# Another order for the 418 tasks of the first stage of an attention and two-layer MoE kernel

## The chip, the cores and the metric

The kernel runs on one core of a Trainium2 chip. The metric is the time of one execution on the device in microseconds; the number before is the median of 3 runs. One further execution was recorded by the hardware profiler; all rows below come from it.

## The reference

Attention with a window (plain for the first half of the heads, dilated by 4 for the second), its output as the input of a gated layer, whose output goes through a second layer with a leaky activation. All in float32.

```python
def _attn_ref(q, k, v):                        # 4 batches, 8 heads, 576 rows, 64 columns
    scores = scale * np.matmul(q, k.transpose(0, 1, 3, 2))
    ...                                        # window 32; heads 4 to 7: window 128, every 4th
    attn = np.exp(scores - np.max(scores, axis=-1, keepdims=True))
    attn = attn / (np.sum(attn, axis=-1, keepdims=True) + 1e-09)
    return np.matmul(attn, v)

def _moe_ref(x, w_gate, w_val, w_out):         # x: 2304 x 512, inner width 1536
    gate = 1.0 / (1.0 + np.exp(-(x @ w_gate)))
    return gate * (x @ w_val) @ w_out

def _moe2_ref(x, w_in, w_out, alpha):          # inner width 2048
    h = x @ w_in
    g = np.maximum(h, 0.0) + alpha * np.minimum(h, 0.0)
    return g @ w_out
```

## The kernel before

A large product is done in float16 with two halves of each operand: a high half (the value scaled by a power of two and rounded to float16) and a low half (what is left). Three products, high x high, high x low and low x high, are summed in PSUM. Every weight is therefore prepared on the chip before TensorE can use it: its bits are put together, a bound of its rows is summed, a power of two is made of that, and high and low halves are written.

The kernel has a first stage, which is a text (`FIRST`, line 1562 on) of 418 tasks, and then loops over the batches b = 1 to 3 and over the second layer, with a planner (`prepare`) that puts the second layer's weights between their products. The first stage covers the attention of batch 0 (`hb` 0 and 1: plain and dilated heads), of batch 1 (`hb` 2 and 3) and the start of batch 2 (`hb` 4), all weights of the gated layer, its products for batch 0, and the first three gate and value blocks of batch 1.

Inside `tc.manual_schedule()` (line 1309 on) the order of the text is the order of the instructions: `run` walks through it and calls one function for each task, and each function issues instructions on one or several engines. Each engine works off its own queue strictly in the order of issue, and semaphores tie the queues together. So a task that stands earlier in the text stands earlier on every engine that it uses, and an instruction that waits holds all those behind it on its engine.

The tasks, with the engines on which they issue:

- `lqk hb`, `lv hb`, `lgv m`, `lo d r`: loads, issued by SP's queue (lines 246, 247, 252, 499, 532). `lgv m` loads 512 KB of gate and 512 KB of value weights. Words of weights and v share 8 slots (pool `yp`); a load waits on SP's queue until a slot comes free, and the loads behind it wait with it.
- `dec m`, `odec d r ...`: VectorE puts the words of a block together, three instructions for each 512 KB (lines 180, 184, 188); the last two read two SBUF tensors.
- `wb m`, `xb hb`, `obd d h`: ACT sums squares (line 195). `wsum`, `xsum`, `osum`, `alpha`: TensorE sums over partitions with a column of ones (line 149). `wpow`, `xpow`, `opow`: VectorE (157, 161) and GpSimd (165) make the power of two.
- `spl m i e`, `ospl d h e`: the two halves of a weight block. With e = 1, ACT writes the high half (172) and VectorE the low one (173). With e = 0 or none, ACT scales the source in place (205) and writes the high half (206), and GpSimd subtracts (169).
- `qkm hb c` (TensorE, 302 to 316), `qks` (VectorE), `exp` (ACT, 362 or 368), `rs` (VectorE), `pm hb c e` (row scaling of the probabilities, 381: GpSimd for e = 0, VectorE for 1), `tr` (VectorE, 399), `phi` (ACT, 403), `plo hb i e` (subtraction, 169, GpSimd for 0, VectorE for 1), `vhi` (ACT, 272), `vlo` (VectorE, 275), `pvm` and `pv32` (TensorE, 430 and 445), `pvx hb half pair` (ACT 172 and VectorE 173, the two halves of x).
- `g b m i`, `v b m i`: half i of the gate and the value product of block m and batch b on TensorE (582), 12 matmuls. `sig` (ACT, 595), `mul` (VectorE, 600), `half b m e` (ACT 610, then the subtraction 169 on GpSimd for 1 or none, on VectorE for 0).
- `orow d r e`: row scaling of w_out (199; GpSimd for e = 0, VectorE for 1). `o b d p`: a quarter of an output product on TensorE (627), 18 matmuls. `oy`: its way to DRAM. `wgs`, `gs`: small scalings on GpSimd (488). `warm n bank`: n products of zeros on TensorE.
- `prep n`: a call of the planner.

The two functions behind a split, and the one behind a half:

```python
    def split_weight(hi, lo, src, s, on_dve=0):                # line 201
        if on_dve:
            return split_act(hi, lo, src, s)                   # ACT 172, VectorE 173
        nc.scalar.activation(src, src, AF.Copy, scale=s)       # ACT 205
        nc.scalar.activation(hi, src, AF.Copy)                 # ACT 206
        rest(nc.gpsimd, lo, src, hi)                           # GpSimd 169

    def gv_halves(b, m, pool=True):
        ...
        nc.scalar.activation(t[:, 0, :], gf, AF.Copy)          # ACT 610
        rest(nc.gpsimd if pool else nc.vector, t[:, 1, :], gf, t[:, 0, :])
```

Of the kernel before, what the change touches and what calls it, by code (L numbers as in the profile page):

```python
# [1572 lines left out]
4; v 0 2 1; dec 5; g 0 3 0; qks 2 1; wpow 4; wb 5; wsum 5 0; g 0 3 1; qks 2 2; spl 4 0; spl 4 1 1; half 0 0 1; wpow 5;
mul 0 2; exp 2; v 0 3 0; dec 6; wgs 3; sig 0 3; v 0 3 1; xpow 1; spl 5 0 1; lgv 8; wb 6; spl 5 1 1; g 0 4 0; wsum 6; v
0 4 0; wgs 4; half 0 2 1; mul 0 3; lgv 10; wpow 6; spl 6 0; g 0 4 1; sig 0 4; spl 6 1; dec 7; wgs 5; g 0 5 0; wb 7;
half 0 3; v 0 4 1; wsum 7; rs 2; g 0 5 1; lgv 9; sig 0 5; wpow 7; g 0 6 0; mul 0 4; wgs 7; spl 7 0; pm 2; v 0 5 0; dec
8; v 0 5 1; tr 2; spl 7 1; g 0 6 1; wb 8; wgs 6; v 0 6 0; wsum 8; half 0 4; wpow 8; dec 9; sig 0 6; vhi 2; g 0 7 0;
mul 0 5; lv 4; phi 2; v 0 6 1; spl 8 0; lqk 3; g 0 7 1; plo 2; spl 8 1 1; wb 9; sig 0 7; lgv 11; mul 0 6; vlo 2; half
0 6 1; half 0 5 1; g 0 8 0; wsum 9 0; lo 0 2; v 0 7 0; lo 0 1; wpow 9; g 0 8 1; dec 10; pvm 2 0; pvx 2 0 1; spl 9 0;
spl 9 1 1; wgs 8; v 0 7 1; wb 10; wsum 10; mul 0 7; v 0 8 0; pvx 2 0 0; wpow 10; sig 0 8; dec 11; spl 10 0 1; spl 10  # L1580
1; v 0 8 1; g 0 9 0; half 0 7 1; wb 11; pvm 2 1; wsum 11; g 0 9 1; pvx 2 1 0; v 0 9 0; odec 0 0 1 2; wpow 11; wgs 9;
orow 0 0 0; v 0 9 1; lo 2 0; orow 0 1 1; pvx 2 1 1; spl 11 0; orow 0 2 0; lo 2 2; qkm 3 0; lo 1 1; qks 3 0; spl 11 1
1; qkm 3 1; mul 0 8; wgs 10; g 0 10 0; xb 4; vhi 3; obd 0 1; obd 0 0; odec 1 0 1; lo 3 1; osum 0; half 0 8 1; qkm 3 2;
sig 0 9; opow 0; v 0 10 0; g 0 10 1; mul 0 9; v 0 11 0; vlo 3; half 0 9 0; wgs 11; v 0 10 1; lo 1 2; odec 1 2; ospl 0
0 1; qks 3 2; qks 3 1; lo 2 1; orow 1 2 0; sig 0 10; lo 3 2; orow 1 0 1; mul 0 10; orow 1 1 0; v 0 11 1; g 0 11 0; g 0
11 1; ospl 0 1; obd 1 0; lqk 4; obd 1 1; osum 1; o 0 0 0; exp 3; odec 2 0 1 2; opow 1; sig 0 11; orow 2 2 0; orow 2 1
1; mul 0 11; orow 2 0 1; o 0 0 1; rs 3; ospl 1 0 1; half 0 11 1; obd 2 1; obd 2 0; pm 3; osum 2; ospl 1 1; o 0 0 2;
# [89 lines left out]
```

## Time and profile before

| | us |
|---|---|
| median of 3 runs | 870.41 (869.15 to 870.77) |
| span of the profiled execution | 870.0 |
| TensorE (PE) busy | 830.0 (95%) |
| VectorE (DVE) busy | 618.3 (71%) |
| ACT busy | 440.7 (51%) |
| GpSimd (POOL) busy | 286.7 (33%) |

"Busy" is the union of an engine's instruction spans. The profile gives the granted clock of TensorE as a share of full speed, which is 2.4 GHz; its other level is 1.2 GHz, so a mean of 0.93 over a stretch is 14% of its time at the low level. Matmuls overlap, so the time of a run of them is read from start to start. A group of instructions is listed with its line, the engine, the operation, the tiles (written<-read), shapes and count, its busy time and the mean of one, then the idle time of the engine just ahead of them and what ended it.

### The profile page before, as it was taken

To read this page: it belongs to the slowest core of one execution; us is meant where nothing else is said; L and a number is where in the kernel's file an instruction comes from. 1 tells how busy PE (TensorE), PEld (TensorE's weight loads), DVE (VectorE), ACT (ScalarE), POOL (GpSimd) and SP (SyncE) were. 2 spreads that over 40 slices of the span, in tenths; PEclk is the share of its full clock that TensorE was granted. 3 is DMA by queue.
4 is the path that set the end of the run, shared out by engine and by line. 5 is a ranking of instruction groups with operands and counts; after the bars stand their busy time and mean duration, and the time that the engine had idled before them with its cause. 6 is when DMAs were issued, how large, how long until landed. Compare 5 with 4: busy or idle time off the path is not lost.

```text
span 870.0 us, 21031 instructions
## 1 busy us (share of the span) xinstructions
PE 830.0 (95%) x8994; PEld 686.7 (79%) x8994; DVE 618.3 (71%) x1031; ACT 440.7 (51%) x730; POOL 286.7 (33%) x261
## 2 busy tenths in 40 slices
...
GB/s 323 286 194 124 229 100 207 15 173 102 92 95 169 139 136 119 50 68 264 301 166 223 342 214 221 337 241 218 308 203 212 243 210 194 225 309 194 122 230 73
DMA packets 85181, 166.91 MB, mean 192 GB/s; under 512 B 5344, under 2 KB 57696, under 8 KB 85088
## 3 DMA queue, kind: packets, MB, share of 16 engines
...
## 4 chain that ended last, share of the span: by engine, by line
PE 76%; DVE 13%; ACT 5%; DMA 4%; issue 2%; POOL 1%; SPq 0%; ACTq 0%; DVEq 0%
PE banks L582 27%; PE banks L1204 18%; PE banks L959 17%; PE banks L627 11%; DVE plain L188 2%; DVE plain L184 2%; DVE plain L180 2%; PE banks L430 1%; PE banks L316 1%; DMA words<-w_out 1%; DMA words<-w_gate 1%; ACT junk L195 1%; DVE plain L199 1%; DMA w_i<-wi_dram 1%; DVE g_g L1045 1%
## 5 line engine op out<-in xcount | busy, mean ns | idle before, releaser
L582 PE MATMUL banks<-xh,w_gv 128*128 128x288 f16 x2304 | 295.5, 290 | 3.1 <-DVE gf L600 2.3
L582 PEld LDWEIGHTS <-w_gv 128*128 128x128 f16 x2304 | 226.1, 99 | 63.3 <-issue 3.2
L959 PE MATMUL banks<-yh,w_i 128*128 128x256 f16 x1536 | 187.1, 273 | 5.1 <-DMA w_i<-wi_dram 1.6
L959 PEld LDWEIGHTS <-w_i 128*128 128x128 f16 x1536 | 150.0, 98 | 24.0 <-issue 3.3
L627 PE MATMUL banks<-gt,w_o 128*128 128x288 f16 x1152 | 147.0, 288 | 0.3 <-POOL gt L169 0.2
L627 PEld LDWEIGHTS <-w_o 128*128 128x128 f16 x1152 | 112.0, 98 | 29.4 <-issue 0.4
L1204 PEld LDWEIGHTS <-g_gv 128*128 128x128 f16 x780 | 76.3, 98 | 8.8
L1204 PE MATMUL banks<-w,g_gv 128*128 128x256 f16 x612 | 75.5, 273 | 0.0
L997 ACT ACTIVATE neg<-banks 128x512 f32<-128x512 f32 x72 | 42.8, 594 | 57.2 <-DVE banks L1017 40.8
L1055 POOL TENSOR_TENSOR yh<-temp_y 128x512 f32<-128x512 f32 x16 | 26.5, 1659 | 125.7 <-DVE temp_y L1005 121.0
L600 DVE SCALAR_TENSOR_TENSOR gf<-banks,sg 128x576 f32<-128x576 f32 x48 | 36.0, 751 | 38.9 <-PE banks L582 27.3
L165 POOL TENSOR_SCALAR sc<-sc 128x1 f32<-128x1 f32 x35 | 11.4, 326 | 157.7 <-DVE sc L161 157.7
L1204 PEld LDWEIGHTS <-g_g 128*128 128x128 f16 x564 | 55.2, 98 | 6.4
L169 POOL TENSOR_TENSOR gt<-gf,gt 128x576 f16<-128x576 f32 x24 | 36.8, 1533 | 63.5 <-ACT gt L610 63.3
L195 ACT ACTIVATE junk<-plain 128x1024 bf16<-128x1024 f32 (+1 forms) x36 | 36.2, 1006 | 40.3 <-DVE plain L199 28.3
L595 ACT ACTIVATE sg<-banks,sc 128x576 f32<-128x576 f32 x48 | 35.3, 735 | 38.1 <-PE banks L582 27.7
L610 ACT ACTIVATE gt<-gf 128x576 f16<-128x576 f32 x48 | 32.3, 676 | 41.3 <-DVE gf L600 41.3
L188 DVE SCALAR_TENSOR_TENSOR plain<-words,plain 128x512 uint32<-128x512 uint32 x68 | 50.8, 767 | 1.2
L184 DVE SCALAR_TENSOR_TENSOR plain<-words,plain 128x512 uint32<-128x512 uint32 x68 | 50.2, 759 | 1.2
L1204 PE MATMUL banks<-w,g_g 128*128 128x256 f16 x396 | 48.3, 273 | 0.0
L1005 DVE SCALAR_TENSOR_TENSOR temp_w<-neg,sc,banks 128x256 f32<-128x256 f32 x64 | 27.8, 475 | 25.1 <-ACT neg L997 25.1
L1045 DVE SCALAR_TENSOR_TENSOR g_gv<-temp_w,sc,g_gv 128x256 f16<-128x256 f32 (+1 forms) x37 | 26.0, 711 | 27.6 <-ACT g_gv L1041 27.6
...
## 6 DMA issues: line engine op xcount, KB each, us to landing
...
```

The source lines that it names most:

```text
L169: engine.tensor_tensor(out=lo, in0=src, in1=hi, op=ALU.subtract)
L184: nc.vector.scalar_tensor_tensor(out=d, in0=hi, scalar=0xC0000000, in1=d, op0=ALU.bitwise_and, op1=ALU.bitwise_or)
L188: nc.vector.scalar_tensor_tensor(out=d, in0=lo, scalar=29, in1=d, op0=ALU.logical_shift_right, op1=ALU.bitwise_or)
L195: nc.scalar.activation(junk[:, :src.shape[1]], src, AF.Square, accum_out=dst)
L582: nc.tensor.matmul(ps[:, h, :], lhsT=a, rhs=x_[:, H2 * h:H2 * h + H2], start=(kk == 0 and i == 0), stop=(kk == KD - 1 and i == 2),)
L595: nc.scalar.activation(halves(sg), ps, AF.Sigmoid, scale=sgx[b][:, m:m + 1])
L600: nc.vector.scalar_tensor_tensor(out=halves(gf), in0=ps, scalar=2.0 ** -15, in1=halves(sg), op0=ALU.mult, op1=ALU.mult)
L627: nc.tensor.matmul(ps[:, h, :], lhsT=a, rhs=x_[:, H2 * h:H2 * h + H2], start=(m == 0 and z == 0), stop=(m == M1 - 1 and z == 2),)
L959: nc.tensor.matmul(o, lhsT=h, rhs=l, start=(new and v == 0 and q == 1), stop=(q == total_), skip_group_check=True,)
L997: nc.scalar.activation(t[:, :2 * n], src[:, :2 * n], AF.Relu, scale=-1.0)
L1045: nc.vector.scalar_tensor_tensor(out=h[:, 1], in0=x_, scalar=s_al, in1=h[:, 0], op0=ALU.mult, op1=ALU.subtract)
L1204: nc.tensor.matmul(ps[:, H4 * t:H4 * t + H4].rearrange("p (c f) -> p c f", c=2), lhsT=a, rhs=x_, start=(first and k == 0 and t == 0 and z ...
```

## The change

`FIRST` gets another order. No other line of the kernel differs. Apart from the place, 39 of the 418 tasks change their engine argument:

- From GpSimd to VectorE: `spl` 0 0, 0 1, 1 0, 3 0, 3 1, 4 0, 6 0, 6 1, 7 0, 7 1, 8 0, 10 1, 11 0 (with one ACT instruction less each); `ospl` 0 1; `half` 0 0, 0 4, 0 5, 0 6, 0 7, 0 10, 1 1; `orow` 0 0, 0 2, 1 1, 3 0, 3 2; `plo` 1 1, 2, 3; `pm` 1 1.
- From VectorE to GpSimd: `spl` 1 1 and 4 1 (with one ACT instruction more each), `half` 0 9, `orow` 0 1.
- Written out but the same: `spl 9 0`, `half 0 3`, `ospl` 1 1 and 2 1, `plo 4`.

The text starts with the loads, decodes and bounds of weight blocks 0 and 1, which stood behind the loads of q, k and v before. `alpha` moves from ahead of `opow 3` to behind `pvx 3 1`, and some gate and value products of batch 1 (`g 1 2`) stand between the output products of batch 0.

The diff, cut:

```diff
 FIRST = """
-lqk 0 3; warm 6 2; warm 8 5; lqk 1 3; qkm 0 0; qks 0 0; qkm 0 1; exp 0 0; qks 0 1 1; qkm 0 2; lv 0; exp 0 1; lv 1; rs
-0 0; qks 0 2 1; qkm 1 0 4; exp 0 2; lgv 0; rs 0 1; pm 0 0 0; qks 1 0; pm 0 1 0; tr 0 0; exp 1 0; tr 0 1; rs 0 2; lal;
-xb 0; pm 0 2 0; lgv 1; lgv 3; qkm 1 1 5; qks 1 1; qkm 1 2 0; rs 1 0; lqk 2; exp 1 1; tr 0 2; pm 1 0 0; qks 1 2 1; rs 1
-1; xb 1; exp 1 2; pm 1 1 0; pv32 0 0 6; lgv 2; dec 0 0; xsum 0 0; rs 1 2; pm 1 2 0; xpow 0; tr 1 1; pv32 0 1 4; vhi 1;
-tr 1 0; phi 1 1; lv 3; dec 0 1; warm 14 3; plo 1 1; lgv 6; pvx 0 0 1; tr 1 2; pvx 0 0 0; wb 0; phi 1 2; vlo 1; lv 2;
-wsum 0; phi 1 0; pvx 0 1 0; plo 1 0 0; plo 1 2 0; wpow 0; pvm 1 0; pvx 0 1 1; dec 1; pvm 1 1 4; spl 0 0; pvx 1 1 1;
-spl 0 1; g 0 0 0; pvx 1 0 0; pvx 1 0 1; lgv 4; wb 1; wsum 1; qkm 2 0; wpow 1; pvx 1 1 0; spl 1 0; wgs 0; g 0 0 1; dec
-2; g 0 1 0; wgs 1; spl 1 1 1; lgv 5; dec 3; wb 2; v 0 0 0; wsum 2 0; sig 0 0; qkm 2 1; lgv 7; wpow 2; spl 2 0 1; spl 2
...
-0; lv 5; ospl 2 1; obd 3 1; o 0 1 2; oy 0 0; orow 3 0 0; o 0 2 0; orow 3 1 1; obd 3 0; pvm 3 0; o 0 1 3; osum 3;
-alpha; opow 3; pvx 3 0 1; o 0 2 1; pvx 3 0 0; pvm 3 1; ospl 3 0 1; pvx 3 1 0; ospl 3 1 1; o 0 3 0; o 0 2 2; pvx 3 1 1;
-qkm 4 0; oy 0 1; qkm 4 1; qks 4 0; qkm 4 2; qks 4 1; qks 4 2; o 0 2 3; o 0 3 1; g 1 0 0; prep 3; g 1 0 1; exp 4; o 0 3
...
+warm 6 2; lgv 0; dec 0 0; dec 0 1; wb 0; lgv 1; warm 8 5; dec 1; wb 1; lqk 0 3; qkm 0 0; qkm 0 1; wsum 0; qks 0 0; qkm
+0 2; lqk 1 3; qkm 1 0 4; wpow 0; qks 0 1 1; exp 0 0; qkm 1 1 5; qks 0 2 1; exp 0 1; rs 0 0; pm 0 0 0; lv 0; qks 1 0;
+wsum 1; rs 0 1; qks 1 1; lv 1; pm 0 1 0; qkm 1 2 0; wpow 1; exp 0 2; qks 1 2 1; exp 1 1; rs 0 2; exp 1 0; pm 0 2 0; tr
+0 1; xb 0; rs 1 0; tr 0 2; tr 0 0; lgv 2; pm 1 0 0; tr 1 0; warm 14 3; rs 1 1; pm 1 1 1; exp 1 2; lgv 3; lqk 2; rs 1
+2; xb 1; pm 1 2 0; lal; tr 1 1; xsum 0 0; lv 3; lgv 6; xpow 0; tr 1 2; spl 0 0 1; spl 0 1 1; pv32 0 0 6; vhi 1; phi 1
+0; vlo 1; pvx 0 0 1; pvx 0 0 0; lv 2; phi 1 1; plo 1 1 1; pv32 0 1 4; pvx 0 1 0; plo 1 0 0; pvm 1 0; pvx 0 1 1; phi 1
+2; plo 1 2 0; spl 1 0 1; pvm 1 1 4; dec 2; lgv 4; g 0 0 0; pvx 1 0 1; pvx 1 1 1; spl 1 1 0; pvx 1 0 0; wb 2; wsum 2 0;
+wpow 2; g 0 1 0; pvx 1 1 0; wgs 0; g 0 0 1; dec 3; g 0 1 1; spl 2 0 1; xb 2; spl 2 1 1; sig 0 0; qkm 2 0; wgs 1; v 0 0
...
+exp 2; g 0 4 1; rs 2; half 0 2 1; wb 7; pm 2; wpow 6; v 0 3 1; lgv 8; wsum 7; mul 0 3; wpow 7; spl 6 0 1; tr 2; v 0 4
...
+1; ospl 2 1 0; obd 3 0; pvm 3 0; orow 3 2 1; pvx 3 0 0; pvx 3 0 1; obd 3 1; o 0 2 0; o 0 2 1; o 0 2 2; o 0 2 3; osum
+3; g 1 2 0; pvm 3 1; opow 3; ospl 3 0 1; o 0 3 0; o 0 3 1; ospl 3 1 1; pvx 3 1 0; pvx 3 1 1; g 1 2 1; oy 0 2; alpha;
+prep 3; prep 6; g 1 0 0; qkm 4 0; qkm 4 1; xpow 2; sig 1 2; qks 4 0; o 0 3 2; g 1 0 1; o 0 3 3; qks 4 1; v 1 0 0; v 1
+0 1; oy 0 3; qkm 4 2; g 1 1 0; sig 1 0; mul 1 0; v 1 1 0; v 1 1 1; qks 4 2; g 1 1 1; vhi 4; exp 4; sig 1 1; vlo 4; rs
+4; mul 1 1; half 1 1 0; pm 4; half 1 0 0; v 1 2 0; v 1 2 1; prep 6; lqk 5; mul 1 2; tr 4; phi 4; plo 4 0 0
 """
```

## Rows read from the trace of the kernel before

**Rows 1.** Busy time by stretch: start:end, length, each engine's busy (instructions), clock, DMA.

```profile
0.00:40.40 40.40, 30.04 (x610) 20.78 (x611) 27.62 (x62) 22.74 (x66) 12.65 (x19) 0.86 0.96 328
40.40:172.80 132.40, 113.08 (x1371) 86.08 (x1369) 115.69 (x194) 83.10 (x129) 69.71 (x69) 0.93 0.43 143
172.80:206.40 33.60, 33.60 (x336) 27.01 (x329) 22.61 (x37) 17.82 (x26) 6.21 (x5) 1.00 0.48 164
206.40:870.00 663.60, 653.30 (x6690) 552.79 (x6687) 452.38 (x741) 316.99 (x510) 198.13 (x168) 1.00 0.55 195
```

**Rows 2.** Chain that ended last, in order of time: start, us, what.

```profile
126.07 0.43 DVE plain L180
...
172.86 4.52 PE banks L627 x36
177.38 2.42 PE banks L316 x72
...
189.47 1.47 PE banks L582 x12
...
193.22 16.91 PE banks L582 x138
```

**Rows 3.** Groups on VectorE from 40.4 to 175.1, shapes apart.

```profile
L188 DVE SCALAR_TENSOR_TENSOR plain<-words,plain 128x512 uint32<-128x512 uint32 x32 | 24.4, 804 | 0.0
L184 DVE SCALAR_TENSOR_TENSOR plain<-words,plain 128x512 uint32<-128x512 uint32 x32 | 22.3, 740 | 0.0
L180 DVE TENSOR_SCALAR plain<-words 128x512 uint32<-128x512 uint32 x32 | 18.7, 625 | 1.8 <-DMA words<-w_out 1.7
L173 DVE SCALAR_TENSOR_TENSOR w_gv<-plain,sc,w_gv 128x512 f16<-128x512 f32 x10 | 9.8, 993 | 2.9 <-ACT w_gv L172 2.7
...
L275 DVE SCALAR_TENSOR_TENSOR vh<-vc,sc,vh 128x1152 f16<-128x1152 f32 x2 | 4.3, 2134 | 0.0
...
L837 DVE TENSOR_SCALAR sc<-alpha_sb 128x16 f32<-128x16 f32 x1 | 2.3, 2335 | 0.0
...
L839 DVE TENSOR_SCALAR sc<-sc 128x16 f32<-128x16 f32 x1 | 1.0, 1021 | 0.0
```

**Rows 4.** Single instructions in order of time: start, us, engine, line, tiles, shapes.

```profile
6.46 0.33 PE L302 MATMUL banks<-mask_sb 128*128 128x384 bf16 x1
...
26.77 1.40 DVE L275 SCALAR_TENSOR_TENSOR second<-vc,sc,second 128x1152 f16<-128x1152 f32 x1
...
40.40 3.08 PE L582 MATMUL banks<-xh,w_gv 128*128 128x288 f16 x13
...
41.06 1.56 POOL L169 TENSOR_TENSOR w_gv<-plain,w_gv 128x512 f16<-128x512 f32 x1 [1.26 <-ACT w_gv L206]
41.52 1.64 DVE L184 SCALAR_TENSOR_TENSOR plain<-words,plain 128x512 uint32<-128x512 uint32 x1
43.09 0.68 DVE L188 SCALAR_TENSOR_TENSOR plain<-words,plain 128x512 uint32<-128x512 uint32 x1
44.29 0.75 DVE L173 SCALAR_TENSOR_TENSOR w_gv<-plain,sc,w_gv 128x512 f16<-128x512 f32 x1
```

**Rows 5.** Groups on GpSimd from 40.4 to 175.1, shapes apart.

```profile
L169 POOL TENSOR_TENSOR gt<-gf,gt 128x576 f16<-128x576 f32 x11 | 16.7, 1524 | 9.4 <-ACT gt L610 9.3
L169 POOL TENSOR_TENSOR w_gv<-plain,w_gv 128x512 f16<-128x512 f32 x12 | 16.3, 1358 | 11.3 <-ACT w_gv L206 11.3
...
L169 POOL TENSOR_TENSOR s<-pt,s 128x1152 f16<-128x1152 f32 x2 | 5.5, 2774 | 1.4 <-ACT s L403 1.4
```

**Rows 6.** DMA of the first 60 us: GB/s in 40 slices of 1.5 us.

```profile
GB/s 0 172 320 362 355 370 364 357 396 404 370 352 336 357 341 350 369 407 411 370 356 378 371 345 389 184 48 0 0 16 289 373 92 378 249 11 0 52 356 289
```

**Rows 7.** Waits from 40.4 to 175.1: engine, line, who was waited for, us, times, longest.

```profile
DVE sc L157 <- PE banks L149: 4.3, 2, 3.0
DVE xh L173 <- ACT xh L172: 3.8, 2, 2.9
...
DVE pt L399 <- POOL s L381: 3.1, 1, 3.1
```

More of the change, by code (lines that the diff above doesn't have):

```diff
@@ L1568 @@
-wsum 0; phi 1 0; pvx 0 1 0; plo 1 0 0; plo 1 2 0; wpow 0; pvm 1 0; pvx 0 1 1; dec 1; pvm 1 1 4; spl 0 0; pvx 1 1 1;
-spl 0 1; g 0 0 0; pvx 1 0 0; pvx 1 0 1; lgv 4; wb 1; wsum 1; qkm 2 0; wpow 1; pvx 1 1 0; spl 1 0; wgs 0; g 0 0 1; dec
-2; g 0 1 0; wgs 1; spl 1 1 1; lgv 5; dec 3; wb 2; v 0 0 0; wsum 2 0; sig 0 0; qkm 2 1; lgv 7; wpow 2; spl 2 0 1; spl 2
-1 1; v 0 0 1; wb 3; g 0 1 1; wgs 2; mul 0 0; wsum 3; wpow 3; spl 3 0; v 0 1 0; sig 0 1; v 0 1 1; lo 1 0; g 0 2 0; spl
-3 1; v 0 2 0; g 0 2 1; dec 4; mul 0 1; qks 2 0; xb 2; xb 3; wb 4; qkm 2 2; sig 0 2; lo 0 0; xsum 1; half 0 1 1; wsum
@@ L1573 @@
[L1573 to L1587, printed above, removed]
@@ L1588 @@
-half 0 10 1; opow 2; o 0 1 0; gs 1; lo 3 0; odec 3 0 1 2; tr 3; ospl 2 0 1; o 0 0 3; orow 3 2 0; o 0 1 1; phi 3; plo 3
-0; lv 5; ospl 2 1; obd 3 1; o 0 1 2; oy 0 0; orow 3 0 0; o 0 2 0; orow 3 1 1; obd 3 0; pvm 3 0; o 0 1 3; osum 3;
-alpha; opow 3; pvx 3 0 1; o 0 2 1; pvx 3 0 0; pvm 3 1; ospl 3 0 1; pvx 3 1 0; ospl 3 1 1; o 0 3 0; o 0 2 2; pvx 3 1 1;
-qkm 4 0; oy 0 1; qkm 4 1; qks 4 0; qkm 4 2; qks 4 1; qks 4 2; o 0 2 3; o 0 3 1; g 1 0 0; prep 3; g 1 0 1; exp 4; o 0 3
-2; lqk 5; oy 0 2; xb 5; sig 1 0; v 1 0 0; rs 4; pm 4; xsum 2; tr 4; o 0 3 3; xpow 2; v 1 0 1; vhi 4; vlo 4; oy 0 3;
@@ L1593 @@
-phi 4; mul 1 0; g 1 1 0; g 1 1 1; v 1 1 0; g 1 2 0; half 1 0 0; sig 1 1; v 1 1 1; g 1 2 1; plo 4; prep 6; v 1 2 0; mul
-1 1; prep 6; lv 6; sig 1 2; v 1 2 1; mul 1 2; half 1 1
+warm 6 2; lgv 0; dec 0 0; dec 0 1; wb 0; lgv 1; warm 8 5; dec 1; wb 1; lqk 0 3; qkm 0 0; qkm 0 1; wsum 0; qks 0 0; qkm
+0 2; lqk 1 3; qkm 1 0 4; wpow 0; qks 0 1 1; exp 0 0; qkm 1 1 5; qks 0 2 1; exp 0 1; rs 0 0; pm 0 0 0; lv 0; qks 1 0;
+wsum 1; rs 0 1; qks 1 1; lv 1; pm 0 1 0; qkm 1 2 0; wpow 1; exp 0 2; qks 1 2 1; exp 1 1; rs 0 2; exp 1 0; pm 0 2 0; tr
@@ new lines @@
+0; dec 4; wb 3; wsum 3; wpow 3; wgs 2; qks 2 0; v 0 0 1; spl 3 0 1; spl 3 1 1; lgv 5; wb 4; g 0 2 0; wsum 4; qkm 2 1;
+wgs 3; sig 0 1; mul 0 0; wpow 4; xb 3; v 0 1 0; v 0 1 1; g 0 2 1; v 0 2 0; v 0 2 1; dec 5; spl 4 0 1; mul 0 1; spl 4 1
+0; half 0 0 0; wb 5; dec 6; qkm 2 2; wsum 5 0; sig 0 2; g 0 3 0; lgv 7; wpow 5; qks 2 1; g 0 3 1; v 0 3 0; spl 5 0 1;
+spl 5 1 1; half 0 1 1; wb 6; lgv 10; wgs 5; mul 0 2; sig 0 3; xsum 1; lgv 9; wgs 4; qks 2 2; wsum 6; dec 7; g 0 4 0;
+exp 2; g 0 4 1; rs 2; half 0 2 1; wb 7; pm 2; wpow 6; v 0 3 1; lgv 8; wsum 7; mul 0 3; wpow 7; spl 6 0 1; tr 2; v 0 4
@@ new lines @@
+0; g 0 5 0; half 0 3 1; v 0 4 1; xpow 1; spl 6 1 1; sig 0 4; v 0 5 0; mul 0 4; g 0 6 0; spl 7 0 1; spl 7 1 1; vhi 2; g
+0 6 1; phi 2; dec 8; v 0 5 1; g 0 5 1; wgs 6; lo 0 0; lo 0 1; wb 8; dec 9; wsum 8; sig 0 5; wpow 8; plo 2 0 1; lo 1 0;
+wgs 7; g 0 7 0; wb 9; wgs 8; mul 0 5; spl 8 0 1; spl 8 1 1; vlo 2; sig 0 6; v 0 6 0; wsum 9 0; half 0 4 0; v 0 6 1; g
+0 7 1; wpow 9; pvm 2 0; g 0 8 0; dec 10; mul 0 6; sig 0 7; spl 9 0 0; lgv 11; pvx 2 0 0; v 0 7 0; spl 9 1 1; lo 1 1;
+half 0 5 0; g 0 8 1; wb 10; lo 0 2; lv 4; dec 11; wsum 10; wpow 10; sig 0 8; half 0 6 0; v 0 7 1; v 0 8 0; mul 0 7;
```

9 lines of the change are left out of this document (added).

## The prediction, on record before the changed kernel ran

> **What bounds the kernel now.** I read the stretches first [rows 1]. Their boundaries are three moments on TensorE: 40.4 us, where it begins the second half of the first gate block (`g 0 0 1`, [rows 4]); 172.8, where it begins `o 0 3 0`; and 206.4, where the first stage's last matmul (`v 1 2 1`) ends, nine half blocks of 1.47 us behind 193.22 [rows 2]. From 172.8 on TensorE is busy 33.60 of 33.60 and then 653.3 of 663.6 us at a granted clock of 1.00: behind 172.8 there is nothing to win but TensorE work that is moved ahead of it. Between 40.4 and 172.8 it is busy 113.1 of 132.4 us at a clock of 0.93. So 19.3 us are idle and 0.07 x 132.4 = 9.3 us are clock: 28.6 us lost, the ceiling of this stretch for any order.
>
> VectorE paces that stretch: 115.7 of 132.4 us busy [rows 1]. Its time splits three ways. (a) Hold-ups: the groups of [rows 3] have means above what the same forms take alone in [rows 2, 4]: L188 (804-680) ns x32 = 4.0 us, L184 (740-680, the same form) x32 = 1.9, L180 (625-430) x32 = 6.2, L173 on w_gv (993-750) x10 = 2.4, L275 (2134-1400) x2 = 1.5; together 16.0. [Rows 4] show one case: an L184 that starts beside a GpSimd subtraction (41.06 to 42.62) takes 1.64 instead of 0.68. GpSimd ran 69 instructions there [rows 1], 37 of them large by the tasks of the order (23 are the two first groups of [rows 5]), so one large operation cost VectorE 16.0/37 = 0.43 us. (b) Waiting: 132.4-115.7 = 16.7 us. (c) Free work: 115.7-16.0 = 99.7 us.
>
> **The change part by part.**
>
> *Loads and start.* Blocks 0 and 1 of the gate and value weights (4 x 512 KB) go ahead of q and k on SP's queue. The DMA engines move some 365 GB/s once they run [rows 6], so 2.1 MB cost 5.75 us: `qkm 0 0` moves from 6.46 [rows 4] to about 12.2. In exchange VectorE has words to decode at 4.3 us at best (0.13 MB of mask and the first 0.5 MB at the rates of those slices), 5.5 taken, and decodes both blocks while q and k arrive. At `g 0 0 1` the old order is still inside `dec 2` (the L184 at 41.52, [rows 4]); the new one has it done, and beside it three w splits, `plo 1 1` and `pm 1 1`: 2 x (0.43+0.68+0.68) = 3.6, 3 x 0.75, and for the other two, a third of the width of L275's 1.40 each, 1.0 together; 6.9 us more VectorE work than the 27.6 us busy of [rows 1]. 5.5+27.6+6.9 = 40.0 with no wait; less 1 for GpSimd operations that are gone, plus 2 for waits, makes 41 us (bounds 40 and 46.1, the last being all of the 5.75 us on top of 40.4). By the clock the start gains nothing, but VectorE stands one block further.
>
> *VectorE's free work from there to `ospl 3 0`, which releases `o 0 3 0`.* Out of the stretch go `dec 2` 3.6, `alpha` 2.3+1.0 by its two long steps [rows 3] (it moves behind `ospl 3 1`), two w splits 1.5, one half 0.75 and one row scaling 0.7: 9.9. New on VectorE are ten w splits 7.5, one w_out split 0.75, six halves 4.5 (each as a split), five row scalings 3.4 (0.68, another two-input form of 512), and `plo 2` and `plo 3`, which no row shows on VectorE: GpSimd takes 2.77 for one [rows 5], VectorE 1.40 for L275, also two-input and 1152 wide, which I take, 2.8. Sum 19.0, net +9.1: 108.8.
>
> *What GpSimd gives back.* 16 of the 37 large operations stay: 16 x 0.43 = 6.9 instead of 16.0 us (bounds 5 and 10). One split moved costs VectorE 0.75 and returns 0.43, so by itself a move is a small loss on VectorE; it pays through ACT (L205 and L206 become one L172) and the shorter way to TensorE.
>
> The Trainium skill (SBUF — State Buffer, "Who interferes with whom") says that GpSimd and a VectorE instruction with two SBUF inputs share a port pair in turns: whichever starts first holds it for its whole instruction, and the other blocks. The rows agree in kind (that L184 lost 0.96 us). At the rule's full price each of the 21 moved operations would return some 1.36 instead of 0.43 us, and the sum would lie 19 us lower, past the ceiling of the stretch.
>
> *VectorE's waits.* Now: 4.3 for TensorE's column sums, 3.8 for ACT's x splits, 3.1 for GpSimd's row scaling ahead of `tr 2` [rows 7], 2.7 for ACT ahead of ten w splits and 1.7 for w_out words [rows 3]. The longest sum wait, 3.0 of the 4.3, is `alpha`'s and goes with it; the words' wait goes, since `lo 1 0` to `lo 2 2` are queued behind slots that come free earlier; the second I halve; the third stays; the fourth grows with 18 splits at 0.27 to 4.9. 1.3+1.9+3.1+4.9 = 11.2; 11 taken (bounds 6 and 16.7).
>
> `o 0 3 0` then starts at 41+108.8+6.9+11 = 167.7, not 172.8. TensorE alone could be there sooner: its own work from `g 0 0 1` was 113.1-9.3 = 103.8 us at full clock, and a few us more are queued there in the new order. VectorE comes last.
>
> *Tail.* Behind the start of `o 0 3 0` the old order has 33.6 us of TensorE work, the new one 4 parts of `o`, 11 half blocks and 3 `qkm`: by [rows 2] 4 x 2.26 + 11 x 1.47 + 2.42 = 27.6. `alpha`'s sum stands on TensorE's queue behind `g 1 2 1`, 2 x 2.26+1.47 = 6.0 us into the tail; VectorE reaches it after `ospl 3 1` (0.75), two `pvx` of the same kind and the 3.3 us, some 5.6: level, nothing is paid.
>
> The stage ends at 167.7+27.6 = 195.3 instead of 206.4, 11.1 us earlier. Behind it the same 663.6 us follow (`prep` is called as often, so the planner stands where it stood). Span 870.0-11.1 = 858.9; the median of the timed runs is 870.41, 0.4 above this span: 859.3, so **859**.
>
> **The rivals.**
>
> *A, attention late.* The bytes of q and k decide, not VectorE: `g 0 0 1` at 46.1 and everything behind it with it, 859.3+5.1 = 864. For it: the DMA engines move 320 to 411 GB/s in every slice from 3 to 36 us [rows 6], so what is put ahead delays what follows. Against: in those 40.4 us VectorE was busy 27.6, part of it with decode that now lies ahead of attention.
>
> *B, the waits move with the work (slower).* GpSimd waits 11.3+9.3 = 20.6 us for ACT's high halves [rows 5]. It has nothing else to do; VectorE, taking over those subtractions in order, would hold decode behind each. If half of that comes over, the waits are 16.7+10.3 = 27 and the stage ends at 41+108.8+6.9+27+27.6 = 211.3: 875. It turns slower once hold-ups and waits exceed 206.4-41-108.8-27.6 = 29.0 us, where I have 17.9 and the old order 32.7. Against: the ten splits that VectorE already does waited 0.27 us each.
>
> *C, nothing moves.* What VectorE gains TensorE loses again in new places (sums queued ahead of ready matmuls, clock): 870, within 1.7.
>
> **How the numbers follow.** Forecast 0.62 (850 to 864), A 0.18 (864 to 868), B 0.12, C 0.08. Low end 40+108.8+5+6+27.6 = 187.4, span 851.0, 850 in round numbers; high end 46.1+108.8+6.9+14+27.6 = 203.4, span 867.0, 868. That leaves B and C out, 2 in 10. 0.2% is 1.7 us, about what a measurement of this kernel can tell from no change: faster 0.82 (forecast, A and the edge of C), same 0.06, slower 0.12.
>
> **What would show it.** Right: from `g 0 0 1` to `o 0 3 0` TensorE loses (idle and clock) near 17 us, not 28.6; `dec 2` is done before `g 0 0 1`; the means of L180, L184 and L188 are near 520, 710 and 730 ns; GpSimd's large operations in the stage are fewer by 26; `o 0 3 0` starts near 168 and the stage ends near 195. Wrong: L173 and L169 on VectorE wait for ACT by more than 10 us (B); `g 0 0 1` comes behind 44 us (A); TensorE has gaps of several us ahead of L149 while VectorE idles (C); or TensorE idles behind the stage, so that the 663.6 us grow.

## The result: 861.2 us, and the profile after

| | before | changed |
|---|---|---|
| median of the comparison on one chip | 871.38 (14 runs) | 861.23 (859.96 to 862.7, 6 runs) |
| ratio to before, 95% interval | | 0.9883 [0.9864, 0.9901] |
| ratio in an earlier comparison | | 0.9906 [0.9877, 0.9935], from 861.15 and 862.88 |
| profiled execution, span | 870.0 | 858.2 |
| first stage ends (`v 1 2 1` on TensorE) | 206.4 | 194.58 |
| behind it | 663.6 | 663.6 |

The forecast was 859 us with a range of 850 to 868. The median is 861.2: faster by 1.2%, inside the range, 2.2 us above the point. The profiled execution took 859.96 us for a span of 858.2. In the earlier comparison two more executions ran in a slow state, at a mean granted clock of 0.935 and 0.747 instead of 0.98, and took 880.3 and 1074.92 us; neither is in a ratio.

The busy time of the changed kernel in the stretches of [rows 1], with the same boundaries (`g 0 0 1` begins at 45.60, `o 0 3 0` at 166.75, `v 1 2 1` ends at 194.58):

```profile
0.00:45.60 45.60, 29.10 (x598) 20.30 (x599) 32.57 (x76) 24.84 (x69) 9.75 (x19) 0.85 0.92 314
45.60:166.75 121.15, 111.50 (x1431) 87.52 (x1429) 106.82 (x197) 75.74 (x119) 35.36 (x44) 0.99 0.46 155
166.75:194.58 27.83, 27.83 (x289) 22.23 (x281) 18.16 (x39) 12.62 (x17) 2.78 (x4) 1.00 0.50 163
194.58:858.20 663.62, 653.40 (x6689) 552.64 (x6687) 458.39 (x747) 319.87 (x515) 199.46 (x169) 1.00 0.55 195
```

The start is 5.2 us longer, the middle stretch 11.2 us shorter, the tail 5.8 us shorter, the rest equal. In the middle TensorE loses 121.15-111.50 = 9.7 us idle and 0.01 x 121.15 = 1.2 us of clock, 10.9 us in all, where it lost 28.6 before.

The groups on VectorE from `g 0 0 1` to `ospl 3 0` (45.6 to 168.3; line, shapes, count, busy us, mean ns, idle time ahead of them), against [rows 3]:

```profile
L184 DVE SCALAR_TENSOR_TENSOR plain<-words,plain 128x512 uint32<-128x512 uint32 x30 | 19.2, 681 | 0.0
L188 DVE SCALAR_TENSOR_TENSOR plain<-words,plain 128x512 uint32<-128x512 uint32 x30 | 19.2, 681 | 0.0
L173 DVE SCALAR_TENSOR_TENSOR w_gv<-plain,sc,w_gv 128x512 f16<-128x512 f32 x18 | 14.8, 854 | 0.0
L180 DVE TENSOR_SCALAR plain<-words 128x512 uint32<-128x512 uint32 x29 | 10.9, 421 | 0.0
...
L275 DVE SCALAR_TENSOR_TENSOR vh<-vc,sc,vh 128x1152 f16<-128x1152 f32 x2 | 2.8, 1406 | 0.0
```

The decode takes what it takes alone (680 and 420 ns): its hold-ups are gone, not halved. And the 18 weight splits wait for nothing; what they still lose to hold-ups is (854-740) ns x 18 = 2.1 us, two of them having a GpSimd operation beside them. The same view for GpSimd, against [rows 5], with 6 + 2 operations where there were 11 + 12:

```profile
L169 POOL TENSOR_TENSOR gt<-gf,gt 128x576 f16<-128x576 f32 x6 | 8.5, 1421 | 6.5 <-ACT gt L610 6.5
...
L169 POOL TENSOR_TENSOR w_gv<-plain,w_gv 128x512 f16<-128x512 f32 x2 | 2.3, 1162 | 5.5 <-ACT w_gv L206 5.5
```

VectorE's waits (waited for, us, times, longest), against [rows 7]:

```profile
DVE xh L173 <- ACT xh L172: 4.9, 1, 4.9
DVE sc L157 <- PE banks L582: 2.6, 2, 2.1
DVE w_o L173 <- ACT w_o L172: 2.4, 2, 1.2
DVE gt L169 <- ACT gt L610: 1.3, 1, 1.3
DVE sc L157 <- PE banks L149: 1.2, 2, 0.8
```

Which instructions stand beside GpSimd is seen in single instructions (start, us, what, idle time before):

```profile
59.79 1.16 POOL L169 TENSOR_TENSOR w_gv<-plain,w_gv 128x512 f16<-128x512 f32 x1 [2.60 <-ACT w_gv L206]
59.79 1.71 DVE L173 SCALAR_TENSOR_TENSOR w_gv<-plain,sc,w_gv 128x512 f16<-128x512 f32 x1
75.27 1.39 POOL L169 TENSOR_TENSOR gt<-gf,gt 128x576 f16<-128x576 f32 x1 [2.45 <-ACT gt L610]
75.43 1.35 DVE L374 TENSOR_REDUCE rs<-s 128x18 f32<-128x1152 f32 x1
```

The first pair collides: L173 takes 1.71 us, not the 0.74 that it takes alone. The second does not: L374 takes 1.35 us, as it did in the kernel before. In the changed kernel, 15 large GpSimd operations run in the stretch for 21.6 us in all. Only 5.8 us of that (27%) lie beside VectorE's decode or its instructions with two SBUF inputs; the rest lies beside reads of PSUM, reductions, transposes, small scalings or nothing. Before it was 30.3 of 56.0 us (54%). The Trainium skill (SBUF — State Buffer, "Who interferes with whom") says that on this chip a reduction never contends with GpSimd and that an instruction with two SBUF inputs contends with a GpSimd instruction that reads SBUF; both pairs agree.

### The profile page after: what moved, and what is told of

Same layout as the page of the kernel before. It is cut to its first block, busy times and chain, and to the rows that moved or that the text cites. A ratio compares the mean times of both kernels' runs of the same rounds, so it can differ in the third digit from the quotient of the medians.

```text
span 878.5 us, 21011 instructions
## 1 busy us (share of the span) xinstructions
PE 849.0 (97%) x8994; PEld 696.7 (79%) x8994; DVE 614.7 (70%) x1057; ACT 432.8 (49%) x718; POOL 247.6 (28%) x235
## 4 chain that ended last, share of the span: by engine, by line
PE 81%; DVE 9%; ACT 2%; DMA 1%; issue 1%; POOL 0%; SPq 0%; ACTq 0%; DVEq 0%
PE banks L582 29%; PE banks L1204 18%; PE banks L959 17%; PE banks L627 13%; PE banks L316 2%; PE banks L430 1%; DVE plain L188 1%; DVE plain L184 1%; DMA w_i<-wi_dram 1%; DVE w_gv L173 1%; DVE g_g L1045 1%; DVE plain L199 1%; DVE plain L180 1%; DVE halves L735 0%; ACT g_g L1041 0%
## 5 line engine op out<-in xcount | busy, mean ns | idle before, releaser
L582 PE MATMUL banks<-xh,w_gv 128*128 128x288 f16 x2304 | 301.0, 294 | 3.3 <-ACT sg L595 1.7
L959 PE MATMUL banks<-yh,w_i 128*128 128x256 f16 x1536 | 192.2, 277 | 4.1 <-DMA w_i<-wi_dram 1.4
L959 PEld LDWEIGHTS <-w_i 128*128 128x128 f16 x1536 | 152.0, 99 | 25.9 <-issue 2.5
L627 PE MATMUL banks<-gt,w_o 128*128 128x288 f16 x1152 | 149.4, 292 | 0.1
L1204 PEld LDWEIGHTS <-g_gv 128*128 128x128 f16 x780 | 77.4, 99 | 10.3
L1204 PE MATMUL banks<-w,g_gv 128*128 128x256 f16 x612 | 77.5, 277 | 0.0
L600 DVE SCALAR_TENSOR_TENSOR gf<-banks,sg 128x576 f32<-128x576 f32 x48 | 36.0, 751 | 40.6 <-PE banks L582 30.4
L184 DVE SCALAR_TENSOR_TENSOR plain<-words,plain 128x512 uint32<-128x512 uint32 x68 | 47.4, 717 | 1.2
L188 DVE SCALAR_TENSOR_TENSOR plain<-words,plain 128x512 uint32<-128x512 uint32 x68 | 46.2, 701 | 1.2
L1014 ACT ACTIVATE temp_y<-banks 128x512 f32<-128x512 f32 x32 | 19.0, 595 | 55.2 <-PE banks L959 55.1
```

The lines of the kernel that those rows point to most:

```text
L184: nc.vector.scalar_tensor_tensor(out=d, in0=hi, scalar=0xC0000000, in1=d, op0=ALU.bitwise_and, op1=ALU.bitwise_or)
L188: nc.vector.scalar_tensor_tensor(out=d, in0=lo, scalar=29, in1=d, op0=ALU.logical_shift_right, op1=ALU.bitwise_or)
L582: nc.tensor.matmul(ps[:, h, :], lhsT=a, rhs=x_[:, H2 * h:H2 * h + H2], start=(kk == 0 and i == 0), stop=(kk == KD - 1 and i == 2),)
L600: nc.vector.scalar_tensor_tensor(out=halves(gf), in0=ps, scalar=2.0 ** -15, in1=halves(sg), op0=ALU.mult, op1=ALU.mult)
L627: nc.tensor.matmul(ps[:, h, :], lhsT=a, rhs=x_[:, H2 * h:H2 * h + H2], start=(m == 0 and z == 0), stop=(m == M1 - 1 and z == 2),)
L959: nc.tensor.matmul(o, lhsT=h, rhs=l, start=(new and v == 0 and q == 1), stop=(q == total_), skip_group_check=True,)
```

## How the experiments are read

For each kernel VectorE's time between the starts of `g 0 0 1` and `o 0 3 0` is split as in the forecast. An instruction's own time runs from its start, or the end of its predecessor if that is later, to its end. A form's free time is the median of those with no large GpSimd operation beside them; what those beside one take above it is hold-up; what is left of the stretch is waiting. (The forecast's 16.0 us of hold-ups, from group means, are 15.4 us by this count.) The border between free and hold-ups is good to some 2 us only: with every excess over the free median added up, without those below it, the hold-ups are 17.8 before, 2.2 in the changed kernel, 10.9 in e1, 8.6 in e2, 3.3 in e4, 10.9 in e5 and 5.7 in e8. The differences from the changed kernel stay within 1.5 us of the column's; sum and waits are the same either way. The columns add up to the start of `o 0 3 0` within 0.4 us, except in e9_dec3_early (1.3), where a wait crosses the boundary.

| kernel | median us, ratio [95%] | `g 0 0 1` | free | hold-ups (large GpSimd operations) | waits | `o 0 3 0` | stage end |
|---|---|---|---|---|---|---|---|
| before | 870.41 | 40.4 | 100.1 | 15.4 (37) | 16.7 | 172.8 | 206.4 |
| forecast of the changed kernel | 859 | 41 | 108.8 | 6.9 (16) | 11 | 167.7 | 195.3 |
| changed, e0_after | 861.23, 0.9883 [0.9864, 0.9901] | 45.6 | 105.7 | 1.2 (15) | 14.3 | 166.75 | 194.6 |
| e1_order_only | 874.31, 1.0041 [1.0022, 1.0059] | 45.9 | 91.2 | 9.2 (36) | 32.4 | 178.4 | 206.3 |
| e2_engines_only | 876.54, 1.0058 [1.0037, 1.0080] | 40.1 | 109.7 | 7.7 (16) | 20.3 | 178.2 | 211.8 |
| e3_qk_first | 863.97, 0.9916 [0.9899, 0.9933] | 50.95 | 105.6 | 1.2 (15) | 14.2 | 172.0 | 199.8 |
| e4_splits_back | 864.78, 0.9940 [0.9923, 0.9958] | 45.2 | 100.8 | 1.4 (24) | 23.9 | 171.3 | 199.2 |
| e5_rest_back | 867.93, 0.9972 [0.9958, 0.9986] | 46.6 | 96.6 | 9.4 (27) | 19.8 | 172.3 | 200.1 |
| e6_new_start_only | 872.59, 1.0029 [1.0014, 1.0044] | 46.4 | 95.7 | 13.4 (36) | 17.2 | 173.0 | 206.6 |
| e7_old_start_only | 862.67, 0.9913 [0.9896, 0.9931] | 41.2 | 108.6 | 2.0 (17) | 16.8 | 169.0 | 196.8 |
| e8_beside_decode | 867.87, 0.9965 [0.9952, 0.9977] | 45.8 | 105.9 | 4.4 (15) | 17.6 | 173.5 | 201.3 |
| e9_dec3_early | 866.13, 0.9940 [0.9920, 0.9959] | 51.4 | 102.8 | 1.2 (15) | 19.1 | 173.2 | 201.0 |
| e10_g_first | 861.95, 0.9894 [0.9874, 0.9913] | 47.95 | 104.6 | 0.4 (15) | 15.7 | 168.6 | 196.4 |
| e11_split_then_dec3 | 860.02, 0.9882 [0.9863, 0.9900] | 48.7 | 102.7 | 1.2 (15) | 18.5 | 169.9 | 197.7 |

The positions come from one profiled execution each. Its start wanders: in 0 to 45 us the granted clock was 0.85 in the profile of the changed kernel and 0.74 in that of e8_beside_decode, whose text is the same up to there, and the matmuls of `pvm 1 0` got going at 32.23 and at 33.07. So one or two microseconds between two starts are not read as an effect, and verdicts rest on the timed runs. The profiled executions also lie differently to their medians: 859.96 to 861.23 in the changed kernel, 865.43 to 863.97 in e3 and 863.26 to 860.02 in e11, so their stage ends differ by more than the kernels do. The changed kernel and e1 to e3 were timed against the same runs of the kernel before (median 871.38), the others against runs with medians of 870.0 to 871.4; a difference between kernels of two comparisons is given by the medians and, where it matters, also by the ratios.

## The changed kernel by itself, and its two halves

The changed kernel as it is, to have its profile beside the others:

> The changed kernel once more, unaltered, for a profile at full clock and more pairs. Both theories expect what was measured: some 8 us under the kernel before (861 to 863). The stage should end near 196 to 198, since behind it the same 663.6 us follow.

Measured 861.23. The stage ends at 194.58, before the expected 196 to 198, in an execution 1.3 us under the median. Then the new order with the old engine arguments:

```diff
-spl 0 0 1; spl 0 1 1; ... half 0 4 0; ... orow 0 2 1; ... plo 2 0 1
+spl 0 0; spl 0 1; ... half 0 4; ... orow 0 2 0; ... plo 2
```

> The new order, but every task keeps its old engine (the 39 engine arguments as before; order as in the changed kernel). Theory of the prediction (VectorE stands one block further and waits less; the moves by themselves cost VectorE 0.75 each and return 0.43): the order alone keeps most of the gain, 860 to 866. Rival (GpSimd's hold on the shared port is what was paid for, the moves carry the gain): the order alone gains nothing or loses, 869 to 880, and L180, L184, L188 on VectorE keep means near 625, 740 and 800 ns.

Measured 874.31: slower than the kernel before, though it has the new order whole. The theory of the prediction (860 to 866) failed; the rival's time came, but not all of its means (L180 496, L184 748, L188 751 ns). Of the 39 arguments 34 change the engine; the other five only write out what was there. In the stretch it looks so:

```profile
45.90:178.44 132.54, 114.75 (x1431) 88.99 (x1429) 100.12 (x176) 82.01 (x129) 61.82 (x65) 0.96 0.42 141
```

VectorE has 14.5 us less to do than in the changed kernel, and the stretch is 11.4 us longer: waits are 32.4, not 14.3 us, and hold-ups 9.2, not 1.2. ACT (fourth of the busy times) has 10 instructions and 6.3 us more. What TensorE waits for, in this kernel and then in the changed one:

```profile
PE banks L149 <- ACT junk L195: 10.2, 4, 4.7
```

```profile
PE banks L149 <- ACT junk L195: 4.6, 2, 3.3
```

The sums over partitions wait for ACT's squares, which stand behind ACT's additional passes, and VectorE waits for the sums in its turn. That is one of several ways: VectorE waits 13.7 us for ACT's halves (8.6 in the changed kernel), 7.2 for sums (3.8), 5.8 for TensorE ahead of L600 (0.9) and 3.8 for GpSimd (0). So the order without the engines wins nothing in the stage, which ends at 206.3 as before. That it is even slower lies behind the stage, where 667.7 us follow and not 663.6: TensorE waits 1.2 us for VectorE's L600 and 0.6 for ACT just there. Of the other 2.3 us some 1.9 are longer busy time of TensorE (655.34 us, not 653.40): its granted clock was 0.94 from 590 to 620 us, where the changed kernel had 1.00 in the same piece. Why is open.

The old order with the 39 new engine arguments:

```diff
-spl 0 0; spl 0 1; ... half 0 4; ... orow 0 2 0; ... plo 2
+spl 0 0 1; spl 0 1 1; ... half 0 4 0; ... orow 0 2 1; ... plo 2 0 1
```

> The old order with the 39 new engine arguments. Theory of the prediction: 16 us of moved work come onto VectorE and about 9 us of hold-ups go, so VectorE has up to 7 us more in a stretch that it paces: 870 to 877. Rival (the moves carry the gain): 860 to 866, the decode means down to near 520, 710 and 730 ns and VectorE's waits no longer than before.

Measured 876.54, slower too, inside the 870 to 877 of the prediction's theory. Here the forecast's price of a move can be seen alone: VectorE's free work rises by 9.6 us, hold-ups fall by 7.7, so the moves are a small loss on VectorE, as the forecast said of one split. The other 3.6 us are waits, and one of them is rival B's mechanism, in VectorE's waits of this kernel:

```profile
DVE w_gv L173 <- ACT w_gv L172: 9.1, 7, 3.2
```

In the old order a split on VectorE follows so closely on ACT's half that it waits, 0.5 us for each of 18, with decode queued behind it. In the new order the same 18 splits wait 0.0. The two parts of the change lose 0.4% and 0.6%, and together they win 1.2%.

## Which moves, and why the order needs them

The new order with only the weight splits back on their old engines:

```diff
-spl 3 0 1; spl 3 1 1; ... spl 4 1 0
+spl 3 0; spl 3 1; ... spl 4 1 1
```

> The changed order with only the weight splits back on the engines they had (13 from VectorE to GpSimd with one more ACT instruction each, 2 the other way); halves, row scalings and the rest stay as changed. Whole kernel, nothing left out. Theory 1 (the new order needs the short way of a split, which leaves ACT one pass less and spares GpSimd's 1.2 to 1.4 us): ACT comes late with the squares, TensorE's column sums wait for it, and this step alone gives back more than half of the 13 us between the changed kernel (861.2) and the order alone (874.3): 868 to 872. Theory 2 (only hold-ups count, 0.43 us for each large GpSimd operation, whatever it is): VectorE is rid of 11 x 0.75 = 8.3 us and gets 11 x 0.43 = 4.7 us of hold-ups, so it is no slower than the changed kernel: 858 to 862.

Measured 864.78, 3.6 us slower than the changed kernel (5.0 by the ratios) and between the two theories, in the range of neither. By the terms theory 1's mechanism is there: waits rise from 14.3 to 23.9 us, free work falls by 4.9, hold-ups hardly move (1.4 us with 24 large operations). The size was too high, since I put more than half of the 13 us on it.

The new order with everything but the splits back:

```diff
-half 0 4 0; ... orow 0 2 1; ... plo 2 0 1; ... ospl 0 1 1; ... pm 1 1 1
+half 0 4; ... orow 0 2 0; ... plo 2; ... ospl 0 1; ... pm 1 1 0
```

> The changed order with the splits as changed, but the halves, the row scalings of w_out, the three plo, ospl 0 1 and pm 1 1 back on the engines they had. Whole kernel, nothing left out. Theory 1 (ACT's way of the splits decides): ACT has only one more pass, little is given back: 861 to 865. Theory 2 (hold-ups by count): VectorE is rid of some 11.7 us and gets 19 x 0.43 = 8.2 us: 857 to 861. If the halves and row scalings on GpSimd are what the new order cannot bear (a half that comes late holds the output product): 866 to 870.

Measured 867.93, 6.7 us slower (7.7 by the ratios), in the third of the expected cases. These moves are paid in another coin: hold-ups rise from 1.2 to 9.4 us and waits by 5.5, while free work falls by 9.1; 2.2 us more follow behind the stage (665.8 for 663.6). Of the hold-ups the splits on VectorE, L173, show (960-740) ns x 18 = 4.0 us, L180 2.2:

```profile
L173 DVE SCALAR_TENSOR_TENSOR w_gv<-plain,sc,w_gv 128x512 f16<-128x512 f32 x18 | 16.7, 960 | 2.1 <-ACT w_gv L172 2.1
L180 DVE TENSOR_SCALAR plain<-words 128x512 uint32<-128x512 uint32 x29 | 13.2, 497 | 0.2
```

Hold-ups are not the whole of it. In the chain that ended last GpSimd's own operations now follow one another on the way to w_out's weights:

```profile
138.35 1.28 POOL gt L169
139.63 1.12 POOL w_o L169
140.75 1.45 POOL plain L199
142.20 1.24 POOL gt L169
143.44 1.01 POOL plain L199
```

The same five, 6.1 us, stand in the chain of e1_order_only from 144.54 on; the chain of the changed kernel has no GpSimd operation in the stage. So the halves and row scalings that stay on GpSimd are late themselves, near to the reason that the third case gave. How much of the 6.7 us is hold-up and how much this lateness, these runs do not separate.

So of the 13.1 us between e1_order_only and the changed kernel about a quarter goes with the splits and half with the other moves, 10.3 us together; by the ratios it is 5.0 and 7.7 of 13.7.

The count of large GpSimd operations does not set the hold-up. Each cost 0.42 us before, 0.08 in the changed kernel, 0.06 in e4, 0.35 in e5, 0.26 in e1 and 0.48 in e2. What it goes with is the share of their time that lies beside decode or two-input instructions: 54% before, 27% in the changed kernel, 25% in e4, 41% in e5, 31% in e1, 58% in e2. A direct test is to leave engines and counts alone and only move six GpSimd tasks in the text to directly ahead of a decode (a `half` takes its ACT pass along):

```diff
-spl 5 1 1; half 0 1 1; wb 6; ... wsum 6; dec 7
+spl 5 1 1; wb 6; ... wsum 6; half 0 1 1; dec 7
```

> The changed kernel with six of its GpSimd operations (half 0 1, 0 2, 0 3, 0 8, 0 9 and orow 0 1) moved in the text to directly ahead of the next decode, so that they run beside VectorE's L180, L184 and L188 and not beside its reads of PSUM and reductions. Same engines, same count, same work on each engine. Theory 1 (what stands beside a GpSimd operation on VectorE sets the hold-up): each of the six costs VectorE 0.7 to 1.0 us, hold-ups from the second half of the first gate block to the last output part go from 1.2 to 5 to 7 us, and the time to 864 to 867. Theory 2 (a hold-up by count, whatever stands beside): hold-ups stay near 1 us and the time at 861.

Measured 867.87, 6.6 us slower: 0.9 us above theory 1's range, with hold-ups below its 5 to 7. Now 11.8 of the 24.1 us of GpSimd's operations lie beside the decode or two-input instructions (49%, not 27%), and hold-ups are 4.4 us, 3.2 more, 0.53 for each operation moved. The rest of the loss is something that the edit brought in besides: the halves come later, and VectorE's product has to wait for the buffer that one of them still reads.

```profile
L180 DVE TENSOR_SCALAR plain<-words 128x512 uint32<-128x512 uint32 x29 | 13.1, 494 | 0.0
L600 DVE SCALAR_TENSOR_TENSOR gf<-banks,sg 128x576 f32<-128x576 f32 x12 | 8.9, 751 | 4.4 <-POOL gt L169 3.6 <-PE banks L582 0.4 <-PE banks L149 0.3
```

So place alone, with the count unchanged, brings hold-ups back; but about half of the 6.6 us is that wait of 3.6, not a hold-up.

## The start

The changed kernel with q and k of the first heads ahead of the weights again:

```diff
-warm 6 2; lgv 0; dec 0 0; dec 0 1; wb 0; lgv 1; warm 8 5; dec 1; wb 1; lqk 0 3; qkm 0 0
+warm 6 2; lqk 0 3; lgv 0; dec 0 0; dec 0 1; wb 0; lgv 1; warm 8 5; dec 1; wb 1; qkm 0 0
```

> The changed kernel with one task put elsewhere: the load of q and k of the first heads stands ahead of the load of weight block 0 instead of behind block 1, so the first scores can start near 6.5 instead of 12 us and the weight words come some 5 us later. Theory of the prediction (the sum of VectorE's work sets the start of g 0 0 1): within 1.5 us of the changed kernel. Rival A (the bytes of q and k set it): g 0 0 1 3 to 5 us earlier and the time 3 to 5 us lower.

Measured 863.97, 2.7 us slower than the changed kernel and outside both expectations; `g 0 0 1` comes at 50.95, later and not earlier. What TensorE waits for up to there:

```profile
PE banks L149 <- ACT junk L195: 9.9, 3, 7.0
...
PE banks L302 <- DVE s L348: 3.4, 1, 3.4
```

The scores are early now, but the decodes stand ahead of everything of attention on VectorE's queue, and their words are what comes late. Rival A took the bytes for the cause by themselves; the bytes and the order of VectorE's queue go together, and putting one first without the other costs more.

Then each start with the other rest, joined behind `g 0 0 1`:

```diff
+(tasks of the changed kernel up to g 0 0 1)
+(remaining tasks in the order and on the engines of the kernel before)
```

> The tasks of the changed kernel up to g 0 0 1, then the remaining tasks in the order and on the engines of the kernel before. Whole kernel, nothing left out. If the new start pays only by the VectorE work that it has behind it (some 6.9 us, against a g 0 0 1 that is 5.2 us later), the stage ends about 1.7 us earlier: 868 to 870. If the bytes of q and k behind the weights decide (rival A): 875. If the new start is what makes the rest run well: 862 to 865.

Measured 872.59: 0.3% slower than before. Its `o 0 3 0` (173.0) and stage end (206.6) are those of the kernel before, and 665.0 us follow, not 663.6; why these 1.4 us more is open. In the stage the VectorE work that it has in hand (95.7 us free, not 100.1) only pays for the later start. It lies between the first expectation and rival A's 875.

```diff
+(tasks of the kernel before up to g 0 0 1)
+(remaining tasks in the order and on the engines of the changed kernel)
```

> The tasks of the kernel before up to g 0 0 1, then the remaining tasks in the order and on the engines of the changed kernel. Whole kernel, nothing left out. If the stretch behind g 0 0 1 is where the gain lies (hold-ups 15.4 to 1.2 us) and VectorE's sum decides: 40.4 + 121.2 + 6.9 us of work that the old start leaves undone = 168.5 for o 0 3 0, against 166.75: 862 to 865. If the 5.2 us of the start come out in full: 856. If the new rest needs the block in hand that the new start gives it: 866 to 872.

Measured 862.67, inside the first expectation, and the working holds term by term: `o 0 3 0` at 169.0 for 168.5. The new start is thus worth 1.4 us (2.6 by the ratios, whose intervals overlap a little, so it is not clear of the noise) with the new rest and less than nothing with the old. Most of the gain lies behind `g 0 0 1`.

In the new start VectorE waits 3.06 us for x at 41.07. Two runs tried to fill that wait with `dec 3`:

```diff
-pvx 1 0 1; pvx 1 1 1; ... g 0 0 1; dec 3
+pvx 1 0 1; dec 3; pvx 1 1 1; ... g 0 0 1
```

> The changed kernel with dec 3 ahead of pvx 1 1 1, where VectorE waits 3.1 us for ACT's high half of x, no longer behind g 0 0 1. If VectorE's sum sets the end of the stage, the decode (3.1 us) fills that wait, everything behind comes 2 to 3 us earlier: 858 to 859.5. If the words of block 3 are not there by 38 us, or if the decode delays the halves of x for TensorE, g 0 0 1 comes later by what VectorE gains: 861 to 862.

Measured 866.13, outside both expectations, 4.9 us slower than the changed kernel. VectorE's wait at that place:

```profile
DVE plain L180 <- POOL w_gv L169: 5.8, 1, 5.8
```

Not the words: `dec 3` writes a buffer that `spl 1 1`, one of the two splits that went to GpSimd, still reads. TensorE is behind it all the same: GpSimd had waited 10.3 us for ACT, and ACT 5.8 us for the end of `pvm 1 1`, in whose middle TensorE stops (the last section). So the next run put that split on VectorE again:

```diff
-spl 1 0 1; pvm 1 1 4; ... pvx 1 0 1; pvx 1 1 1; spl 1 1 0; ... g 0 0 1; dec 3
+spl 1 0 1; spl 1 1 1; pvm 1 1 4; ... pvx 1 0 1; dec 3; pvx 1 1 1; ... g 0 0 1
```

> The changed kernel with dec 3 ahead of pvx 1 1 1 as in e9_dec3_early, and spl 1 1 on VectorE directly behind spl 1 0, as in the kernel before, no longer on GpSimd. In e9 the first L180 of dec 3 waited 5.8 us for GpSimd's L169 of spl 1 1, the last reader of the buffer that dec 3 writes. Theory 1 (that buffer is the cause): the wait is gone, dec 3 fills VectorE's wait for x, VectorE is 3.1 us of decode further at g 0 0 1 for 0.75 us of split: 858 to 860. Theory 2 (the words of block 3 come late, or TensorE is what decides at this point): L180 waits again, for a DMA, or g 0 0 1 is later by what VectorE gains: 861 to 863.

Measured 860.02, a ratio of 0.9882 against 0.9883: no change from the changed kernel that these runs can tell. The wait for the buffer was the cause of the loss in e9: `dec 3` begins at 41.52, with no wait. But the gain is not there. TensorE now waits for VectorE's L157 of block 2, and in the chain that ended last this short step stands behind `dec 3` and the halves of x:

```profile
PE banks L582 <- DVE sc L157: 2.3, 1, 2.3
```

```profile
44.71 1.34 DVE xh L173 x2
46.06 0.04 DVE sc L157
...
46.14 5.92 PE banks L582 x24
```

So `g 0 0 1` comes at 48.7, not 45.6, by what VectorE gained, as theory 2 has it; the time lies at theory 1's edge. Behind it VectorE has 3.0 us less free work and 4.2 us more waits, for TensorE's sums above all (L157 waited 3.8 us in the changed kernel and 7.2 here). VectorE still comes last at this point: what fills its gap stands ahead of a step that TensorE waits for.

## Why the prediction was right, and where its steps were off

*What bounds, and the rest.* Right. Nothing moved behind the stage (663.6 us), and the whole gain is in the stretch and the tail. TensorE's loss in the stretch fell further than I said, to 10.9 instead of 17 us. Its own work there is now 111.50-1.2 = 110.3 of 121.15 us, and from 110 us on the chain that ended last runs almost wholly over TensorE, where [rows 2] still had a decode on it; ahead of that VectorE still has most of it from 68 to 110:

```profile
94.52 1.33 DVE vh L275
111.48 7.44 PE banks L582 x48
...
135.91 6.62 PE banks L627 x54
...
155.16 9.03 PE banks L627 x72
```

*Start, 41.* Mis-sized by 4.6 us. The first words came at 5.16 (5.5), VectorE was busy 32.6 us (33.5), but waited 7.8 us where I had added 2. More than half of that is its wait for x behind `pvm 1 1`, 3.06 + 0.99 us. I had put the 2 us down without a row. The products of `pvm` get going at 32.23, where it was 28.93 before, and in the middle of `pvm 1 1` TensorE stood 4.56 us, where it had stood 3.03: it goes on at 38.71, ACT takes the next half of x at 40.23, VectorE at 41.07. By the sign that I had named, a `g 0 0 1` behind 44 us, rival A was right in that its 46.1 is close; it was wrong in the consequence. The lateness did not pass on: `dec 2` was done at 37.31, as forecast, and the stretch was shorter by more than the start was longer.

*Free work, 108.8.* 105.7; e2_engines_only, with the same moves in the old order, has 109.7. The sum of moved instructions was good to 3 us.

*Hold-ups, 6.9.* Here the step itself was wrong, not only a size. I priced a large GpSimd operation at 0.43 us whatever stood beside it, so that 16 of them must cost 5 to 10. They cost 1.2 (2.2 by the larger count), because the new order puts them mostly beside instructions that do not collide. e8_beside_decode shows that the place does it; e4, with 24 operations and 1.4 us, that the count does not. What a pair that does collide costs is seen at 59.79: 0.97 us.

*Waits, 11.* 14.3. The splits' wait, forecast at 4.9, is 0.0, GpSimd's row scaling is not waited for any more (3.1 forecast), but x costs 4.9 (1.9 forecast), sums 3.8 (1.3) and w_out's splits 2.4. The waits of L173 and L169 for ACT come to 8.6 us, under the 10 that would have meant rival B.

*`o 0 3 0`, 167.7; tail, 27.6; stage end, 195.3.* 166.75, 27.83 and 194.58. The sum came out to 1 us because its errors cancel, which is luck: +4.6 -3.1 -5.7 +3.3 = -0.9.

*From span to time.* Mis-sized by 1.4 us. I put 0.4 us between span and time from a median and one span; a single execution lies 1.8 us above its own span (859.96 and 858.2). So the profiled execution of before was one of the slower, and a span of 858.9 meant 860.7, next to the measured 861.2.

*Large operations.* 24 in the stage instead of 51: 27 fewer, 26 forecast. L180, L184 and L188 are at 421, 681 and 681 ns, below the 520, 710 and 730 forecast, for the reason above.

*What carried the gain.* The forecast held that a move is by itself a small loss on VectorE and pays through the short way of a split. e2 bears out the first and e4 the second. What it did not see is that order and engines need each other: each alone is slower than before, and e1 missed the 860 to 866 expected from its theory. Nor did it see that GpSimd's operations could be late themselves, as in e1 and e5. Rival B, at 0.12, is what the engines do in the old order (9.1 us of waits for ACT's halves), and only the order takes them away.
